# Attention and token mixing under one written order: all PSUM banks in one pool, groups of scores ordered singly, loads behind the first q and k

## The chip, the cores and the metric

The kernel runs on one core of one Trainium2 chip. The metric is the time of one execution on the device in microseconds. The kernel before took 212.9 us, the median of three runs (211.02, 212.9 and 214.1). Lower is better.

## What is computed

Two stages, fused. The first is attention over 4 batches, 8 heads, 768 positions and 64 channels, in which a query sees a window of 128 keys and the first 4 keys ("sinks"). The second is one layer of an MLP mixer over the result, read as 4 batches of 768 tokens by 512 channels.

```python
scores = (q @ k.transpose(0, 1, 3, 2)) / np.sqrt(D)          # D = 64
keep = (pos[None, :] < n_sink) | ((rel >= 0) & (rel < window))
a = softmax(np.where(keep, scores, -1e9))
x = (a @ v).transpose(0, 2, 1, 3).reshape(B, S, H * D)       # 4 x 768 x 512
h = np.maximum(x.transpose(0, 2, 1) @ w_tok1, 0) @ w_tok2    # 768 -> 256 -> 768
u = x + h.transpose(0, 2, 1)
out = u + np.maximum(u @ w_ch1, 0) @ w_ch2                   # 512 -> 1536 -> 512
```

All matrix work is in bf16 with sums in float32.

## The kernel before

**Pairs and batches.** Two heads make a pair, so there are 16 pairs, four of each batch. Only two tiles of 128 keys reach a tile of 128 queries, and the four sinks are added as a small matmul of their own.

**Units.** The work of TensorE (PE) is cut into units, and each unit belongs to a stream that is named by a letter. The first attention (pairs 0 to 3) has t (transposition of q or k), m (the additive mask, put into PSUM by a matmul), s (scores), o (sinks' scores and the products with v, `pv`, L686); g and h are the token mixing of batch 0. Pairs 4 to 15 and the token mixing of batches 1 to 3 are made in `attention_and_tokens` (L948) as streams a and k. c holds the 96 units of the first channel product (`v1`, L990, 4 matmuls of 384 columns each), x the units of the second (`whole`, L1145, 3 matmuls of 512 columns each, 24 units in a batch).

In stream a, units are bursts (L408): several pieces joined into one unit. For pair p one burst holds the transposition of pair p + 1 (`transposed`, L544, up to pair 7), scores of group 0 (`scores`, L583) and the sinks' part of the output of pair p - 1 (`sink_values`, L728); two units `values` (L762) follow; a second burst holds scores of groups 1 and 2, and in some pairs the sinks' scores (`score_sinks`, L659) or the transposition of u (`turned_u`, L879). Pieces use parts of the array: transposition, scores of group 0 and the sinks' values 64x128, scores of groups 1 and 2 and turned u 64x64, the sinks' scores 64x32; all other units use the whole array.

Below, "S8,0" is the scores of pair 8, group 0, and "V8" the values of pair 8; "k8", "v8" name loads.

**The order.** ORDERED (L47) is the order of all units on PE. LOADED (L60) is the order of the loads that POOL issues: q, k and v of a pair, w_tok (t0, t1), w_ch1 in four parts (c0 to c3) and w_ch2 in four (d0 to d3). q and k of a pair take two DMAs each. q and k of pairs 0 to 3 are loaded in float32 by SP and cast (on ACT, DVE and, for pair 3, POOL); all other loads cast on their way and are issued by POOL.

**The planner.** `Plan` (L279) runs while the program is built. It walks through ORDERED, and with costs in ns (L251 and in each `Op`) estimates when each unit and each piece of other work could run. From that it chooses the engine and the place in the engine's queue of every eviction, exponential, copy, load and DMA transposition. What is put into an engine's queue runs in that order on the chip: a copy that waits for a late load holds up all that stands behind it on its engine. `ready` (L289) is the time at which what an operation needs is done; `choose` (L304) gives a unit its PSUM banks; `other` (L336) takes the operation that can begin first. Loads are taken in the order of LOADED, with at most 8 DMAs in flight.

**PSUM.** There are eight banks. Before, two pairs of banks (sc, `NSC = 2`) are for scores and masks, and four single banks (mx, `NMX = 4`) for all else. Once the units of the first attention and token mixing are over, mx units may take halves of the sc tiles too (`late`).

**From pair 8 on** (BY_DMA) q and k are transposed by DMAs that SP issues (`turn` in `prepare`, L452), and four columns of each kT are copied to kTs (`sinks_of`, POOL or DVE). `sink_rows` (L776) copies the four sink rows of v of each pair to v_sink; ACT, DVE or POOL may do it. For pairs 0 to 3 one copy, `v_sink` (POOL, after a small load on SP), does this; the load v1 waits for that copy in the planner (L1270), and so do those behind v1 in LOADED; t0 and q4 stand ahead of it.

Of the kernel before, what the change touches and what calls it, by code (L numbers as in the profile page):

```python
# [16 lines left out]
def kernel(  # L17
# [41 lines left out]
    SC_LATE = 0  # L59
# [19 lines left out]
    NSC, NMX = 2, 4  # L79
    LATER = "cxyak"  # L80
# [5 lines left out]
    def bank(tag, *shape, dtype=FP32, slot=None):  # L86

        n = given[tag].pop(0) if slot is None else slot
        if tag == "sc":
            return sc[n]  # L90
        if n < 2 * NSC:
            size = 1
            for x in shape:
                size *= x
            flat = sc[n // 2][:, n % 2].rearrange("p b c d -> p (b c d)")
            flat = (flat if dtype == FP32 else flat.bitcast(dtype))[:, 0:size]
            names = "abc"[:len(shape)]
            return flat.rearrange(
                f"p ({' '.join(names)}) -> p {' '.join(names)}", **{x: v for x, v in zip(names, shape)},
            )  # L100
        return psum.tile([P, *shape], dtype, name=f"ps_{tag}", tag=f"{tag}{n}", bufs=1)
# [79 lines left out]
    keep_warm(7, 2 * NSC)  # L181
# [69 lines left out]
    SEM = 90.0  # L251
    PE_OUT = 190.0
# [10 lines left out]
    class Op:  # L263
        def __init__(self, cost, fn, deps=(), then=(), size=0.0, lag=None, loads=0, traffic=0.0):
            self.cost, self.fn, self.deps, self.then = cost, fn, list(deps), list(then)
            self.done = None
            self.lag = SEM if lag is None else lag
            self.size = size
            self.urgent = 0
            self.loads, self.traffic = loads, traffic  # L270
            self.need = {}
            self.half = False

# [5 lines left out]
    class Plan:  # L279
        def __init__(self):  # L280
            self.free = {"PE": 0.0, "ACT": 0.0, "DVE": 0.0, "SP": 0.0, "POOL": 0.0}
            self.queue, self.landings = 0.0, []
            self.sent = 0.0
            self.half = False
            self.pending = []
            self.held = [()] * (2 * NSC + NMX)
            self.late = False

        def ready(self, op):  # L289
# [6 lines left out]
            return t  # L296
# [7 lines left out]
        def choose(self, op):  # L304

            taken, given, t = set(), {}, 0.0
            for tag in ("sc", "mx"):
                banks = op.need.get(tag, ())
                free = []
                if tag == "sc" and banks:  # L310
                    for n in range(NSC):
                        halves = [self.freed(2 * n), self.freed(2 * n + 1)]
                        if None not in halves:
                            free.append((max(*halves, self.free["PE"]), n))
                elif banks:
# [7 lines left out]
                given[tag] = [f[-1] for f in free[:len(banks)]]  # L323
                t = max([t] + [f[0] for f in free[:len(banks)]])
# [45 lines left out]
        def run(self, units, early):  # L370

            early = len(early)
            units = list(units)
            while units or self.pending:
                self.late = early == 0
# [18 lines left out]
                name, op = units.pop(0)  # L394
                self.commit_pe(op, t)
                early -= name not in LATER

# [54 lines left out]
    def prepare(p):  # L452
# [23 lines left out]
        if p >= BY_DMA:  # L476
# [23 lines left out]
            )  # L500
            plan.pending.append(done["kTs", p])
# [274 lines left out]
    def sink_rows(p):  # L776
# [5 lines left out]
        done["vs", p] = Op({"ACT": 550.0, "DVE": 420.0, "POOL": 600.0}, both, [done["v", p], done["pv", p - NHP]])  # L782
# [165 lines left out]
    def attention_and_tokens():  # L948

        tokens, units = [], []  # L950
        first, last = NHP, len(pairs) - 1
        prepare(first)
        units += [turn(first, n) for n in range(2)]
        for p in range(first, last + 1):
            b, hp = pairs[p]
            pieces = []
            if p < last:
                prepare(p + 1)
                if p + 1 < BY_DMA:
                    pieces.append(transposed(p + 1))  # L960
            pieces.append(scores(p, 0))
            if p > first:
                pieces.append(sink_values(p - 1))
            units.append(burst(*pieces))
            if p > first:
                units += [values(p - 1, i) for i in range(2)]
            pieces = [scores(p, 1), scores(p, 2)]
            if hp == 0 and p > first:
                tokens.append(mix_h(b - 1, 1, 0, NTOK))
                tokens += [mix_u(b - 1, 1, st, 2) for st in range(0, NT, 2)]  # L970
                if p <= BY_DMA:
                    pieces.append(turned_u(b - 1, 1))
            if hp == NHP - 1 and p < BY_DMA:
                pieces.append(turned_u(b, 0))
            if hp % 2 == 0:
                pieces.append(score_sinks(p + 1))
            units.append(burst(*pieces))
            units[-1].then.append(sink_rows(p))
            if hp == 2:
                tokens.append(mix_h(b, 0, 0, NTOK))  # L980
                tokens += [mix_u(b, 0, st, 2) for st in range(0, NT, 2)]
        units += [pv(p, half) for half in range(2)]
        tokens.append(mix_h(b, 1, 0, NTOK))
        tokens += [mix_u(b, 1, st, 2) for st in range(0, NT, 2)]
        return units, tokens
# [284 lines left out]
    loads["v1"][1].deps.append(v_sink)  # L1270
    for name in LOADED.split():
        queue(*loads[name])
# [40 lines left out]
    streams.update(zip("ak", attention_and_tokens()))  # L1313
# [9 lines left out]
    plan.run(units, [u for u in units if u[0] not in LATER])  # L1323
# [35 lines left out]
```

## Time and profile before

| what | before |
|---|---|
| runs shown, us | 211.02, 212.9, 214.1 (median 212.9) |
| profiled execution, us | 211.98 |
| its span, first to last instruction, us | 210.2 |
| TensorE busy, us | 196.1 (93%) |
| ScalarE (ACT) busy, us | 106.1 (50%) |
| VectorE (DVE) busy, us | 103.4 (49%) |
| GpSimd (POOL) busy, us | 73.1 (35%) |
| moved by DMA | 26.28 MB, mean 125 GB/s |
| mean granted clock of TensorE | 0.984 |

The profile is of one execution. The page lists busy time by engine and by 40 slices of the span; the digits are tenths of a slice, and PEclk is the clock that TensorE was granted, in tenths of full speed. The view of stretches gives the same by windows of time. The waits say which engine sat idle for what, with the total in us, the count and the longest. The chain of waits follows the work that ended last back from the end; in order of time its columns are start, length and what ran. A row of a timeline has start, length, engine, line, operation, tiles (out<-in), shapes and count, and in brackets the idle time of the engine ahead of it and what ended it. Line numbers such as L147 are often those of a helper through which all matmuls go, so rows are told apart by their tiles.

### The profile page before, as it was taken

How to read it: one execution, taken by the hardware profiler on the slowest of the kernel's cores; microseconds unless marked ns; L12 is line 12 of the kernel's file. 1: busy time of each engine (PE TensorE's matmuls, PEld its weight loads, DVE VectorE, ACT ScalarE, POOL GpSimd, SP SyncE). 2: the span in 40 equal slices, each digit the busy share in tenths (PEclk: the TensorE clock that was granted, in tenths of full speed). 3: DMA queues.
4: the chain of work that ended last, by engine and by line, in shares of the span. 5: the costliest groups of instructions: out<-in, count | busy, mean ns of one | idle time of the engine just before them, and what ended most of it. 6: DMA issues, size and time to landing. Idle time of an engine off the chain costs nothing.

```text
span 210.2 us, 4834 instructions
## 1 busy us (share of the span) xinstructions
PE 196.1 (93%) x1999; PEld 117.7 (56%) x2017; DVE 103.4 (49%) x228; ACT 106.1 (50%) x184; POOL 73.1 (35%) x110
## 2 busy tenths in 40 slices
PE   6686999999999999929999999999999999999993
PEld 2333688666664655615765655567665455565453
DVE  4666677676496656614656657753422322000222
ACT  4496768877864115347776425458553003774000
POOL 7667967688364967554310040000000000000000
PEclk9999799999999999978999999999999999999999
DMA  6999999999999999999945763220120533000222
GB/s 173 247 282 162 155 167 195 173 157 195 120 175 128 174 229 183 173 155 182 152 53 100 90 159 93 90 57 23 25 50 3 150 102 119 8 0 0 100 103 100
DMA packets 92550, 26.28 MB, mean 125 GB/s; under 512 B 82544, under 2 KB 89584, under 8 KB 92528
## 3 DMA queue, kind: packets, MB, share of 16 engines
q0 software_dynamic: 67232, 11.80, 75.4%
q1 hardware_dynamic: 25296, 14.17, 29.3%
q8 instruction: 16, 0.26, 0.5%
q14 instruction: 6, 0.05, 0.1%
HBM read 26.75 MB, written 6.29 MB: 157 GB/s over the span
## 4 chain that ended last, share of the span: by engine, by line
PE 75%; DMA 16%; POOL 4%; issue 1%; DVE 1%; ACT 0%
PE ps_mx L147 65%; DMA v_aug<-in_v_dram 10%; PE ps_sc L147 9%; DMA q_bf<-in_q_dram 6%; POOL q_bf L132 1%; POOL v_aug L140 1%; PE ps_mx L552 1%; PE ps_mx L150 1%; PE ps_mx L534 0%; POOL w_tok L165 0%; DVE u_sb L856 0%; POOL mask_add L197 0%; POOL mask_add L201 0%; ACT v1T L160 0%; DVE mask_add L191 0%
## 5 line engine op out<-in xcount | busy, mean ns | idle before, releaser
L147 PE MATMUL ps_mx<-uT,w_ch 128*128 128x384 bf16 x364 | 66.1, 331 | 3.7 <-ACT v1T L160 3.7
L147 PE MATMUL ps_mx<-w_ch,v1T 128*128 128x512 bf16 (+2 forms) x285 | 62.8, 361 | 0.9 <-issue 0.2
L160 ACT ACTIVATE v1T<-ps_mx 128x384 bf16<-128x384 f32 x78 | 38.2, 493 | 36.3 <-PE ps_mx L147 34.7
L623 ACT ACTIVATE pT<-ps_sc 128x1024 bf16<-128x1024 f32 (+1 forms) x48 | 44.5, 953 | 19.0 <-PE ps_sc L147 18.6
L147 PEld LDWEIGHTS <-w_ch 128*128 128x128 bf16 x384 | 36.6, 99 | 28.3 <-issue 6.0
L147 PEld LDWEIGHTS <-v1T 128*128 128x128 bf16 x312 | 28.5, 98 | 27.5 <-issue 0.5
L1158 DVE TENSOR_TENSOR o_sb<-ps_mx,u_sb 128x512 f32<-128x512 f32 x22 | 15.2, 691 | 36.1 <-PE ps_mx L147 36.0
L132 POOL DMA_DIRECT2D k_bf<-in_k_dram x24 | 19.9, 834 | 8.6 <-DMA k_bf<-in_k_dram 4.0
L147 PEld LDWEIGHTS <-w_tok 128*128 128x128 bf16 x192 | 18.5, 98 | 5.5
L132 POOL DMA_DIRECT2D q_bf<-in_q_dram x24 | 19.9, 837 | 4.6 <-DMA w_ch<-in_moe_w_ch_dram 2.2
L856 DVE TENSOR_TENSOR u_sb<-ps_mx,x_sb 128x512 bf16<-128x512 f32 x19 | 12.9, 689 | 15.4 <-PE ps_mx L147 15.2
L140 POOL DMA_DIRECT2D v_aug<-in_v_dram x16 | 16.6, 1043 | 9.1 <-ACT v1T L160 3.6
L641 DVE TENSOR_TENSOR pT<-pT,mask_main 128x1024 bf16<-128x1024 bf16 (+1 forms) x24 | 14.4, 619 | 6.4 <-ACT pT L623 6.4
L147 PEld LDWEIGHTS <-pT 128*128 128x128 bf16 x352 | 15.3, 100 | 3.3 <-DMA v_aug<-in_v_dram 0.4
L147 PE MATMUL ps_sc<-qT,kT 64*64 64x192 bf16 (+3 forms) x288 | 15.6, 256 | 0.0
L147 PE MATMUL ps_mx<-v_aug,pT 128*128 128x65 bf16 x308 | 15.0, 197 | 0.0
L147 PE MATMUL ps_mx<-h1T,w_tok 128*128 128x256 bf16 x92 | 13.8, 273 | 0.0
L147 PE MATMUL ps_mx<-x_sb,w_tok 128*128 128x256 bf16 x96 | 11.9, 273 | 0.1
L147 PEld LDWEIGHTS <-kT 64*64 64x64 bf16 (+1 forms) x288 | 6.8, 103 | 8.7 <-issue 6.7
L641 DVE TENSOR_TENSOR pT<-pT,mask_first 128x1024 bf16<-128x1024 bf16 x13 | 8.9, 684 | 5.3 <-ACT pT L623 5.1
L162 DVE TENSOR_SCALAR v1T<-ps_mx 128x384 bf16<-128x384 f32 x13 | 7.2, 555 | 7.2 <-PE ps_mx L147 7.0
L156 POOL COPY kTs<-kT 64x4 bf16<-64x4 bf16 x14 | 2.6, 184 | 23.2 <-DMA kT<-k_bf 18.8
(79 smaller groups left out, 150.5 us busy)
## 6 DMA issues: line engine op xcount, KB each, us to landing
out_dram<-o_sb SPq DMA_DIRECT2D x23, 256.0 KB, 2.2
v_aug<-in_v_dram POOLq DMA_DIRECT2D x16, 192.0 KB, 9.0
w_ch<-in_moe_w_ch_dram POOLq DMA_DIRECT2D x8, 384.0 KB, 9.2
q_bf<-in_q_dram POOLq DMA_DIRECT2D x24, 96.0 KB, 8.4
k_bf<-in_k_dram POOLq DMA_DIRECT2D x24, 96.0 KB, 9.7
q_f<-in_q_dram SPq DMA_DIRECT2D x4, 384.0 KB, 6.7
k_f<-in_k_dram SPq DMA_DIRECT2D x4, 384.0 KB, 7.6
w_tok<-in_moe_w_tok_dram POOLq DMA_DIRECT2D x2, 384.0 KB, 9.6
```

The source lines that it names most:

```text
L132: in_order(nc.gpsimd.dma_start(out=out[:, h], in_=rows[:, h]))
L140: in_order(nc.gpsimd.dma_start(out=v_aug.rearrange("p i t d -> p (i t) d")[:, :, 0:D], in_=v[b].rearrange("h s d -> (h s) d")[2 * hp * S:2 ...
L147: in_order(nc.tensor.matmul(*args, skip_group_check=True, **kwargs))
L150: in_order(nc.tensor.transpose(out, in_, ident))
L156: in_order({"DVE": nc.vector, "POOL": nc.gpsimd}[e].tensor_copy(out=out, in_=in_))
L160: in_order(nc.scalar.activation(out, in_, AF.Relu))
L162: in_order(nc.vector.tensor_scalar_max(out=out, in0=in_, scalar1=0.0))
L552: in_order(nc.tensor.transpose(ps[x][:, n, j], bfs[p, n][rows, j], ident[rows, rows]))
L623: in_order(nc.scalar.activation(part(tiles["pT", p][:, :, ds(2 * g, 2)]), of_keys(tiles["ps_s", p, g])[:, :, 0:width(g)], AF.Exp, scale=scale,
L641: in_order(nc.vector.tensor_tensor(out=pt, in0=pt, in1=m, op=ALU.min))
L856: in_order(nc.vector.tensor_tensor(out=u_part(b, g, s0, n), in0=tiles["ps_u", b, g, s0], in1=x_sb[b][:, s0:s0 + n, c0:c0 + cn], op=ALU.add,))
L1158: in_order(nc.vector.tensor_tensor(out=o_sb.rearrange("p (g c) -> p g c", g=2), in1=u_rows(b, st), in0=tiles["ps_out", b, st].rearrange("p ...
```

## The change

- `NSC = 4` and no `NMX`: all eight banks are four tiles of two banks. A unit of scores or masks takes a tile, and any other unit takes any free bank. `choose` prefers banks that have been free for SLACK (250 ns); scores take low ones first, others high ones. `late`, `LATER` and `SC_LATE` go.
- `attention_and_tokens` returns five streams in place of two: a (scores, each group a unit of its own, 36), b (for each two pairs the sinks' scores, and for each pair the sinks' values and two units of values, 42), e (transpositions of pairs 4 to 7), f (turned u of batch 1) and k (token mixing, as before). The last pair uses sink_values and values in place of two `pv` units. The sink rows of all pairs, and the preparation of all pairs, are put before the planner at the start.
- ORDERED and LOADED are new. All loads of LOADED wait for the v_sink copy in the planner.
- In the planner, an operation can have a margin that is added to the time at which it is ready: 1500 ns for sink_rows, 1000 ns for the kTs copies from pair 8 on. Stores and transpositions by DMA now push back the estimated queue of loads by their full cost, not by 0.6 of it. sink_rows looks up the values unit of four pairs earlier by its name at the time it is needed.

```diff
     ORDERED = (
-        "t0-1 m0-1 s0-1 t2-3 m2 s2 m3 o0 s3 m4 t4 o1 s4 m5 t5 o2 s5 m6 t6 s6 a0 m7 t7 s7 o3 m8 s8 o4 s9-10 a1 m9 "
-        "g0 s11 m10 o5 s12 o6 g1 o7-8 a2 g2-3 h0-1 g4-5 h2-3 a3 g6 h4-7 g7 c0-3 a4 c4-5 a5-6 c6-9 a7 c10-14 a8-10 "
-        "c15-19 k0 a11 c20 k1 c21-23 k2 a12 k3 a13-14 x0-2 a15 x3-7 a16 x8 a17 x9 a18 x10-12 k4 x13-14 k5-6 x15 "
-        "k7 x16-19 a19 x20-23 c24 a20 c25 a21 c26 a22 c27 a23 c28-34 a24-25 c35-36 a26-27 c37 k8 c38-40 k9 c41-42 "
...
+        "t0-1 m0-1 s0 m2 s1 t2-3 s2 m3 s3 m4 o0 s4 m5 t4 s5 o1 t5 o2 m6 t6 s6 o3 m7 t7 s7 m8 o4 s8-10 m9-10 "
+        "s11-12 g0 o5-6 g1 o7-8 g2 e0-1 g3 h0-1 g4-5 h2-3 g6 h4-5 g7 h6 e2 a0 h7 c0-2 b0 a1 c3-5 b1 a2-3 c6-8 b2 "
+        "c9 a4-5 c10-12 b3 c13-14 e3 b4 c15-16 b5 c17 b6 c18-19 e4 a6-7 k0 c20 x0 b7 a8 c21-22 k1 x1 a9 b8 c23 b9 "
+        "k2 x2 b10 a10-11 x3-8 a12-13 b11-13 x9-11 k3 x12 k4 x13 a14 f0 a15 b14 x14 k5-6 x15-17 k7 x18-20 f1 a16 "
+        "b15 x21-22 c24-27 x23 c28 b16 c29-30 b17 c31-34 a17 b18 a18 c35-37 b19-20 c38-39 a19-20 b21 c40-43 k8 "
...
     LOADED = (
-        "t0 q4 v1 k4 k5 v2 q5 v3 t1 v4 k6 c1 c0 c2 q6 v6 d0 k7 q7 v5 q10 q8 c3 d2 d3 k8 q9 d1 v7 k9 k10 q11 q12 "
-        "q13 v12 v8 k11 v10 k13 k15 v9 q14 q15 k12 v11 v13 v14 k14 v15"
+        "v1 t0 v3 v2 t1 q4 k4 c3 q5 c0 k5 c2 v4 d1 k7 k6 v5 c1 q6 q7 d0 v6 q8 d2 k9 k8 v7 d3 q9 k11 v8 q13 k10 v9 "
+        "k15 v12 q10 k14 q11 k12 q12 v10 v11 v13 q14 v14 k13 q15 v15"
     )
...
-    NSC, NMX = 2, 4
-    LATER = "cxyak"
+    NSC = 4
...
-            return t
+            return t + op.margin
...
+            ats = [self.freed(n) for n in range(2 * NSC)]
...
-                        halves = [self.freed(2 * n), self.freed(2 * n + 1)]
+                        halves = ats[2 * n:2 * n + 2]
                         if None not in halves:
-                            free.append((max(*halves, self.free["PE"]), n))
+                            free.append((max(max(halves) + SLACK, self.free["PE"]), n, max(halves)))
                 elif banks:
-                    for n in range(2 * SC_LATE if self.late else 2 * NSC, 2 * NSC + NMX):
-                        at = self.freed(n)
+                    for n, at in enumerate(ats):
                         if at is not None and n not in taken:
-                            free.append((max(at, self.free["PE"]), n < 2 * NSC, at, n))
+                            free.append((max(at + SLACK, self.free["PE"]), 2 * NSC - 1 - n, at))
...
-                        self.queue = max(self.queue, self.free["SP"]) + 0.6 * op.traffic
+                        self.queue = max(self.queue, self.free["SP"]) + op.traffic
...
+            done["kTs", p].margin = 1000.0
             plan.pending.append(done["kTs", p])
...
-        done["vs", p] = Op({"ACT": 550.0, "DVE": 420.0, "POOL": 600.0}, both, [done["v", p], done["pv", p - NHP]])
+        done["vs", p] = Op({"ACT": 550.0, "DVE": 420.0, "POOL": 600.0}, both, [done["v", p], ("pv", p - NHP)])
+        done["vs", p].margin = 1500.0
         return done["vs", p]
...
+        scored, out, turns, turned, tokens = [], [], [], [], []
+        first, end = NHP, len(pairs)
+        for p in range(first, end):
+            prepare(p)
+            plan.pending.append(sink_rows(p))
+        turns += [turn(first, n) for n in range(2)]
+        turns += [burst(transposed(p)) for p in range(first + 1, BY_DMA)]
+        for p in range(first, end):
+            scored += [burst(scores(p, g)) for g in range(NT // 2)]
+            if p % 2:
+                out.append(burst(score_sinks(p)))
+                for n in (p - 1, p):
+                    out += [burst(sink_values(n)), *(values(n, i) for i in range(2))]
...
-    loads["v1"][1].deps.append(v_sink)
     for name in LOADED.split():
+        loads[name][1].deps.append(v_sink)
         queue(*loads[name])
```

The orders not printed here in full end alike: the second channel product of batch 3 comes last in both.

More of the change, by code (lines that the diff above doesn't have):

```diff
@@ L90, in bank @@
             return sc[n]
[L91 to L101, printed above, removed]
+        size = 1
+        for x in shape:
+            size *= x
+        flat = sc[n // 2][:, n % 2].rearrange("p b c d -> p (b c d)")
+        flat = (flat if dtype == FP32 else flat.bitcast(dtype))[:, 0:size]
+        names = "abc"[:len(shape)]
+        return flat.rearrange(
+            f"p ({' '.join(names)}) -> p {' '.join(names)}", **{x: v for x, v in zip(names, shape)},
+        )
     in_order = tc.keep_in_program_order
@@ L251 @@
     SEM = 90.0
+    SLACK = 250.0
     PE_OUT = 190.0
@@ L322, in choose @@
                     return None, None
-                given[tag] = [f[-1] for f in free[:len(banks)]]
-                t = max([t] + [f[0] for f in free[:len(banks)]])
+                found = free[:len(banks)]
+                t = max([t] + [f[2] for f in found])
+                given[tag] = [f[1] if tag == "sc" else 2 * NSC - 1 - f[1] for f in found]
                 if tag == "sc":
@@ L368, in commit_pe, with run @@
             self.pending.extend(op.then)
[L370 to L372 removed]
+        def run(self, units):
             units = list(units)
             while units or self.pending:
[L375 removed]
                 o = self.other()
@@ L393, in run @@
                 assert t is not None, "no unit can begin"
-                name, op = units.pop(0)
-                self.commit_pe(op, t)
-                early -= name not in LATER
+                self.commit_pe(units.pop(0)[1], t)
     def unit(ns, fn, deps=(), need=None, then=(), half=False):
@@ L948, in attention_and_tokens @@
     def attention_and_tokens():
[L950 to L981, printed above, removed]
@@ L987, in mix_channels @@
+        return scored, out, turns, turned, tokens
     def mix_channels(b):
@@ L1322 @@
         units += [(name, streams[name][n]) for n in range(int(first), int(last or first) + 1)]
-    plan.run(units, [u for u in units if u[0] not in LATER])
+    plan.run(units)
 _INS = ['q', 'k', 'v', 'n_sink', 'window', 'moe_w_tok1', 'moe_w_tok2', 'moe_w_ch1', 'moe_w_ch2']
```

19 lines of the change are left out of this document (10 added, 9 removed), and 9 rows, old and new, of the table ORDERED.

## The prediction

> **What bounds the kernel now.** I read the page first, then the stretches, then the waits and the chain in order of time, and last the timelines of ACT, POOL and PE at the places the chain pointed to. The page:
>
> ```profile
> span 210.2 us, 4834 instructions
> PE 196.1 (93%) x1999; PEld 117.7 (56%) x2017; DVE 103.4 (49%) x228; ACT 106.1 (50%) x184; POOL 73.1 (35%) x110
> ...
> PEclk9999799999999999978999999999999999999999
> DMA  6999999999999999999945763220120533000222
> ```
>
> TensorE is the bound: busy 93% of the span, and no other engine is above 56%. The DMA row matters as much: the DMA engines are nine tenths busy from the second slice (5.3 us) to the twentieth, so for the first half of the span the loads are a second bound, and an order that asks for a load too soon waits. The PEclk row has two dips, in the fifth slice and in the eighteenth and nineteenth. The stretches show what stands there:
>
> ```profile
> 15.00:20.00 5.00, 3.13 (x65) 1.86 (x65) 3.18 (x10) 3.76 (x6) 3.17 (x4) 1.00 2.16 185
> 20.00:25.00 5.00, 5.00 (x71) 2.67 (x69) 3.19 (x9) 2.69 (x4) 4.82 (x7) 0.66 2.26 147
> ...
> 85.00:90.00 5.00, 4.40 (x58) 2.71 (x57) 2.91 (x7) 1.40 (x2) 2.38 (x4) 1.00 1.56 171
> 90.00:95.00 5.00, 1.91 (x7) 0.89 (x7) 1.00 (x2) 2.96 (x7) 3.18 (x4) 0.74 2.11 164
> 95.00:100.00 5.00, 5.00 (x52) 3.07 (x51) 2.05 (x5) 3.31 (x7) 2.03 (x6) 0.92 2.28 174
> ```
>
> The columns are the stretch, its length, busy time of PE, PEld, DVE, ACT and POOL, and the granted clock. PE loses time before 20 us and around 90 us, and each loss is followed by a stretch at a lower clock. From 25 us on, outside 88 to 97, PE is full. The waits name the two losses:
>
> ```profile
> PE ps_mx L147 <- ACT v1T L160: 3.7, 1, 3.7
> PE ps_mx L534 <- DMA q_bf<-in_q_dram: 1.6, 1, 1.6
> ...
> PE ps_sc L147 <- ACT pT L623: 0.2, 1, 0.2
> ```
>
> **Loss A, at 18 us.** Unit a0 turns q of pair 4 and stands in PE's order before the end of the first attention. Its load is late:
>
> ```profile
> 6.32 13.16 DMA q_bf<-in_q_dram
> 19.47 0.14 issue
> 19.61 0.35 PE ps_mx L534 x12
> ```
>
> PE waits 1.6 us, and then runs 20 to 25 at a clock of 0.66, which costs (1 - 0.66) x 5 = 1.7 us. Together 3.3 us.
>
> **Loss B, at 89 us.** On ACT, in order of time:
>
> ```profile
> 86.63 0.49 ACT L160 ACTIVATE v1T<-ps_mx 128x384 bf16<-128x384 f32 x1 [0.72 <-PE ps_mx L147]
> 92.00 0.53 ACT L154 ACTIVATE v_sink<-v_aug 4x65 bf16<-4x65 bf16 x2 [4.88 <-DMA v_aug<-in_v_dram]
> 92.55 0.49 ACT L160 ACTIVATE v1T<-ps_mx 128x384 bf16<-128x384 f32 x1
> ```
>
> ACT took up the copy of sink rows of v (sink_rows, L776) before that load had landed, and sat 4.88 us. Behind it in ACT's queue stood the eviction of a PSUM bank for which PE waited. The load is that of pair 9: its issue is the twelfth of v, and v9 is the twelfth v in LOADED:
>
> ```profile
> 80.91 1.01 POOL L140 DMA_DIRECT2D v_aug<-in_v_dram x1 [0.69 <-DMA v_aug<-in_v_dram]
> ```
>
> The wait costs PE 3.7 us. The lower clock adds (1 - 0.74) x 1.91 x 2 = 1.0 us at 93 to 95 (busy time that ran at half rate there) and 0.08 x 5 = 0.4 us after 95. Together 5.1 us.
>
> **The change, part by part.** Matrix work is the same but for the last pair (two pv units become sink_values and values, under 0.2 us, counted as nothing).
>
> *LOADED.* v9 moves from place 41 of 49 to place 34, v8 from 36 to 31, while the units that use them (V9, V8) stand after nearly the same work as before. SLACK, the margins of 1500 (sink rows) and 1000 (kTs), and the full cost of transposes and stores in the planner's queue move those copies later on their engines. I take loss B as gone: -5.1 us. What is late next is in the rivals.
>
> *The start.* a0 becomes e0, and moves behind the first attention, g1 and g2. Loss A goes, up to -3.3 us, but the loads allow less. v1, t0 and the rest now wait for the v_sink copy (L156 on POOL, 9.12 to 9.73). Before, t0 and q4 were issued ahead of it, from 4.69:
>
> ```profile
> 4.69 0.83 POOL L165 DMA_DIRECT2D w_tok<-in_moe_w_tok_dram  x1
> 5.50 1.75 POOL L132 DMA_DIRECT2D q_bf<-in_q_dram  x2
> 9.12 0.61 POOL L156 CAST v_sink<-v_sink_f 128x520 bf16<-128x520 f32 x1 [1.86 <-DMA v_sink_f<-in_v_dram]
> ...
> 18.43 1.02 POOL L140 DMA_DIRECT2D v_aug<-in_v_dram  x1
> ...
> 44.32 2.25 POOL L165 DMA_DIRECT2D w_ch<-in_moe_w_ch_dram  x3
> ```
>
> On POOL's queue some five loads fit between 9.73 and the cast of q_f of pair 3 (at 16.23, where POOL idled 2.2 us), so that cast is not put off. The pace of loads: I count a load of v, or of a pair's q or k, as one share (192 KB) and a weight as two (384 KB). From v2 (18.43) to c3 (44.32) 22 shares went out in 25.9 us, 1.18 us each. With three shares (t0, q4) in by 19.5, and the same volume (v1, t0) then if the engines are as full as before, the new list has k5 (place 11, 15 shares) in at 19.5 + 12 x 1.18 = 33.6 and c1 (place 18, 25 shares) at 45.4. The users: e2 stands 5.6 us of PE work later than a2, which held the same transposition:
>
> ```profile
> 29.85 0.46 PE ps_mx L552 x24
> ...
> 38.14 0.65 PE ps_mx L147 x4
> ...
> 46.61 3.38 PE ps_mx L147 x20
> ```
>
> (thirteen units of g and h that ran behind a2 now run ahead), so e2 comes at 35.4 less the gain; c12, the third of the five v1 units in the last row (47.9), has 1.0 us less work ahead (the transposition of pair 6 and one values unit now come behind it), and comes at 46.9 less the gain. So k5 allows a gain of 1.8 us and c1 one of 1.5. My pace counts a weight as two full shares, which is too dear for weights, so both land a little sooner. I take -2.0 us, between 1.5 and 3.3.
>
> *Single groups.* Bursts joined pieces of one tiling of the array. I counted changes between the shapes 128x128, 64x128, 64x64 and 64x32 along both orders: 84 before, 90 after (full to small 75 and 67; among the small ones 9 and 23). Price, from the same 16 score matmuls:
>
> ```profile
> 56.05 0.49 PE L147 MATMUL ps_sc<-qT,kT 64*64 64x192 bf16 x16
> 56.47 0.40 PE L147 MATMUL ps_mx<-qT,kTs 64*32 64x512 bf16 x4
> ...
> 63.98 0.49 PE L147 MATMUL ps_sc<-qT,kT 64*64 64x192 bf16 x16
> 64.28 0.60 PE L522 MATMUL ps_mx<-ident,u_sb 64*64 64x64 bf16 x48
> ```
>
> Before a change of shape they take 0.42 us from start to start, before work of the same shape 0.30: 0.12 us a change. Of the 14 more changes among small shapes all are between 64x128 and 64x64, a pair that has no row here. If they are free the sum is -8 x 0.12 = -1.0 us; at the nearest row's price it is 6 x 0.12 = +0.7 us. I take +0.7, as the change to 64x32 is as much a change among small shapes. The Trainium skill speaks against this part of the change: its page "TensorEngine Tiling (Array Packing)", section "Tiling Modes", says that a change of tiling mode, not merely of tile, drains TensorE. By that rule every one of the 14 is paid, +0.7 us; the row to 64x32 agrees with it, and for the pair in question no run here shows it yet.
>
> *One pool of banks.* PE's waits before hold one of 0.2 us for a bank of scores and loss B, so at most 0.2 us is to be won. The cost: sink_values now takes two banks until its values units have run (b15 to b17 is 7 us of work), and c24 to c27 and c72 to c75 hold four until the last unit of the batch before has read v1T. Eight banks cover both by my count; if not, PE waits for one eviction of 0.5 us at each. I take zero.
>
> *Sum.* 210.2 - 5.1 - 2.0 + 0.7 = 203.8 us of span. The profiled execution took 211.98 us, 1.8 more than its span, so 205.6 us. It lies 0.9 below the median of the runs shown (212.9); I leave that, since its two losses are DMA waits that differ from run to run.
>
> **The rivals.**
>
> *kT of pair 8 is late.* k8 is the 26th load in both lists, after equal shares (35), so it lands near 19.5 + 32 x 1.18 = 57.3 in both. S8,0 (a16 before, a12 after) has 0.3 us less work ahead:
>
> ```profile
> 68.16 0.39 PE L147 MATMUL ps_sc<-qT,kT 64*128 64x256 bf16 x4
> ...
> kT<-k_bf SPq DMA_TRANSPOSE x8, 6.8
> ```
>
> With the gain it comes at 65.9. The transposition takes 6.8 us in the median, and k9 now lies ahead of k8: 57.3 + 6.8 = 64.1, and one more transposition ahead of it makes it 65 to 68. A wait of 2 us, with a stretch at half clock of 1 us or so, gives 208.5 us. Before, it was hidden by 2 us; 20%.
>
> *The loads start late.* If the DMA engines were not full from 5 to 10 us without t0 and q4, their three shares are lost: 3 x 1.18 = 3.5 us, the gain at the start turns into a loss, and the time is 209.1 us. For it: every load of the list waits for 9.73. Against: q_f and k_f fill the engines then (first slice six tenths, with hardly another load). 15%.
>
> *Nothing mended.* Another sink copy blocks ACT as v9's did: 205.6 + 5.1 = 210.7 us. Each batch has four such copies. 5%.
>
> *Slower: POOL's own queue.* POOL copies kTs after a DMA transposition, and loads are issued behind it:
>
> ```profile
> POOL kTs L156 <- DMA kT<-k_bf: 18.8, 4, 7.7
> ```
>
> and the chain has S10,0 at
>
> ```profile
> 97.80 0.33 PE ps_sc L147 x4
> ```
>
> Before, most of these waits came after the last load. In the new list 23 loads stand behind k8. If POOL takes the copies of pairs 9, 8, 10 and 11 and sits 6.8 us at each, of which the loads in flight cover about half, the list slips by 4 x 3.4 = 13.6 us. q10 (47 shares: 71.4, with some 10 us of transposes and stores 81, and its own transposition 87) then comes at 101 for S10,0 at 90 (97.8 in the row, less loss B, 0.3 and 2.0), and PE waits 11 us and runs slow for 1.7: 218 us. It decides once the list slips by more than 3 us, and makes a slower kernel from 15. Against: the copies have a margin and may go to DVE. 10%.
>
> **How the numbers follow.** Forecast (202.5 to 207.5) 50%, kT8 20%, late loads 15%, nothing mended 5%, POOL 10%. The low end is the sum with free changes (-1.7) and the whole of loss A (-1.3). The range goes from 202.5 to 211.0: it leaves out POOL and little else. About 2% is what a measurement of this kernel can tell from no change: 208.6 and 217.2. Faster: the forecast, three fifths of kT8, a fifth of late loads, 65%. Slower: POOL, 10%. Within: 25%.
>
> **What would show it.** Right: no wait of ACT for v_aug over 1 us before 100 us; no PE wait for q_bf near 18 us and a clock of 1.00 from 20 to 25; the first c unit (38.1 before, and 1.1 us less work ahead now) at 36 or less; PE without a gap over 0.5 us from 25 us to the end. Wrong: a PE gap over 2 us anywhere, with a lower clock behind it; PE waiting for k_bf, w_ch or kT; POOL idle over 3 us for kT ahead of a load; small gaps at each single group that sum to over 2 us.

## The result and the profile after

The changed kernel takes 232.72 us (median of 4 runs, 232.21 to 233.13); the kernel before, beside it on the same chip, 211.96 us (4 runs, 210.84 to 214.1). The ratio is 1.0998 with an interval of 1.0916 to 1.1079: 10% slower. Ratios here leave out executions that ran disturbed, so they need not be the quotient of the two medians.

The profiled execution of the changed kernel took 232.35 us, its span 230.6. Its page:

```profile
span 230.6 us, 4854 instructions
PE 200.3 (87%) x2003; PEld 115.5 (50%) x2021; DVE 107.6 (47%) x240; ACT 100.2 (43%) x176; POOL 71.6 (31%) x106
...
PE   6878987999899989999998988998888798888872
...
PEclk9999999999999999999999999999999999999999
DMA  6999999999999999999077351002104211001212
```

The clock is full in every slice, both dips of before are gone, and yet PE is busy for only 87% of the span (93% before). The row of PE shows where: eights and nines are mixed from end to end, and the second half, where the DMA engines have little to do, is the worse one. The stretches of the changed kernel (columns as in the prediction; the two behind the clock are of the DMA engines):

```profile
15.00:20.00 5.00, 4.12 (x75) 2.44 (x75) 2.85 (x10) 3.88 (x8) 5.00 (x7) 1.00 1.89 177
20.00:25.00 5.00, 4.34 (x68) 3.35 (x68) 2.26 (x5) 3.08 (x4) 4.11 (x7) 1.00 1.91 176
25.00:60.00 35.00, 31.41 (x406) 20.32 (x404) 21.92 (x53) 22.32 (x43) 26.92 (x35) 1.00 1.90 169
...
90.00:95.00 5.00, 4.62 (x46) 2.80 (x44) 2.16 (x5) 1.98 (x5) 1.02 (x2) 1.00 2.02 130
...
100.00:150.00 50.00, 46.41 (x486) 27.13 (x490) 28.23 (x59) 24.19 (x42) 2.93 (x11) 1.00 0.65 90
150.00:200.00 50.00, 43.42 (x281) 24.15 (x283) 14.26 (x26) 13.97 (x29) 0.00 (x0) 1.00 0.17 48
```

From 15 to 25 and from 90 to 95, where before had its two losses, the clock stands at 1.00, and from 90 to 95 PE does 4.62 us of work instead of 1.91. The loss is elsewhere: 3.6 us of idle time from 25 to 60, 3.6 from 100 to 150, 6.6 from 150 to 200. Before, the last two stretches had 0.4 and 0.2 us of it:

```profile
100.00:150.00 50.00, 49.63 (x546) 31.08 (x548) 30.02 (x62) 28.66 (x45) 4.84 (x17) 1.00 0.52 85
150.00:200.00 50.00, 49.79 (x279) 27.52 (x282) 10.05 (x15) 17.82 (x36) 0.00 (x0) 1.00 0.19 59
```

The waits of PE in the changed kernel (total, number, longest):

```profile
PE ps_sc L145 <- DVE o_sb L1139: 6.4, 9, 0.8
PE ps_sc L145 <- ACT v1T L158: 4.6, 12, 0.7
PE ps_sc L145 <- DVE u_sb L853: 3.2, 6, 0.8
```

No wait is long and none is for a load of weights, of k or of kT. PE waits for readers of PSUM: the sum into o_sb, the eviction to v1T, the sum into u_sb. None of these waits is much over 0.8 us; one such reading takes 0.69 us on DVE and 0.49 us on ACT. The end of the kernel, where nothing runs but the last channel product, shows one at a time (timeline of the changed kernel, PE and DVE):

```profile
207.33 5.34 PE L145 MATMUL ps_sc<-w_ch,v1T 128*128 128x512 bf16 x24
...
209.53 0.69 DVE L1139 TENSOR_TENSOR o_sb<-ps_sc,u_sb 128x512 f32<-128x512 f32 x1 [16.17 <-PE ps_sc L145]
...
212.77 0.69 DVE L1139 TENSOR_TENSOR o_sb<-ps_sc,u_sb 128x512 f32<-128x512 f32 x1 [2.55 <-PE ps_sc L145]
213.51 2.75 PE L145 MATMUL ps_sc<-w_ch,v1T 128*128 128x512 bf16 x11 [0.84 <-DVE o_sb L1139]
...
216.30 0.69 DVE L1139 TENSOR_TENSOR o_sb<-ps_sc,u_sb 128x512 f32<-128x512 f32 x1 [2.84 <-PE ps_sc L145]
```

Twelve matmuls make one row tile of the output, and a row tile has a bank of its own. From 209 us on, DVE has nothing to do but to add up finished row tiles. Yet it does not begin when a row tile is finished: it begins when PE's run of matmuls ends (212.67, then 216.26), and PE goes on only when DVE is done (213.46). The compiled program names the PSUM tile. These are four of DVE's instructions in their order, with what each reads and waits for (the brackets name the engines and queues waited for):

```
231 L1139 TensorTensor o_sb_2786<-ps_sc_88,u_sb 128x512 [waits DVE_49,DMAHW4_49,PE_49,Activation_49]
232 L1139 TensorTensor o_sb_2801<-ps_sc_88,u_sb 128x512 [waits DMAHW6_49,DVE_49,PE_49]
233 L1139 TensorTensor o_sb_2816<-ps_sc_88,u_sb 128x512 [waits DMAHW7_49,DVE_49,PE_49]
234 L1139 TensorTensor o_sb_2840<-ps_sc_88,u_sb 128x512 [waits DMAHW0_49,DVE_49,PE_49]
```

The row tiles at the end use the two banks of one tile, ps_sc_88, in turn. In the program's list for PE, the first of the stretches above is 9 matmuls into ps_sc_87 and 15 into ps_sc_88: the last nine of one row tile, all twelve of the next, and three of the one after. Only then does DVE read the row tile that was finished three matmuls earlier, and the fourth matmul of the new one waits for that reading. So PE stops in the middle of a sum, with its own bank in hand: it waits for no free bank. Two engines that use different banks of one tile take turns.

### The profile page after: what moved, and what is told of

It is laid out like the page before. It is cut to its first block, busy times and chain, and to the rows that moved or that the text cites. A ratio compares the mean times of both kernels' runs of the same rounds, so it can differ in the third digit from the quotient of the medians.

```text
span 230.6 us, 4854 instructions
## 1 busy us (share of the span) xinstructions
PE 200.3 (87%) x2003; PEld 115.5 (50%) x2021; DVE 107.6 (47%) x240; ACT 100.2 (43%) x176; POOL 71.6 (31%) x106
## 4 chain that ended last, share of the span: by engine, by line
PE 66%; DVE 14%; ACT 9%; DMA 5%; issue 3%; SPq 0%; POOL 0%; DVEq 0%; POOLq 0%; ACTq 0%
PE ps_sc L145 65%; ACT v1T L158 6%; DVE o_sb L1139 4%; DMA v_aug<-in_v_dram 3%; DVE u_sb L853 3%; DMA v_sink_f<-in_v_dram 2%; DVE v1T L160 2%; DVE x_sb L746 1%; DVE x_sb L706 1%; ACT pT L619 1%; ACT u_sb L152 1%; DVE pT L637 1%; ACT pT_sink L671 1%; DVE h1T L160 0%; ACT uT L152 0%
## 5 line engine op out<-in xcount | busy, mean ns | idle before, releaser
L145 PE MATMUL ps_sc<-w_ch,v1T 128*128 128x512 bf16 (+2 forms) x297 | 68.1, 362 | 10.2 <-DVE o_sb L1139 5.5
L145 PE MATMUL ps_sc<-uT,w_ch 128*128 128x384 bf16 x384 | 70.2, 326 | 5.9 <-ACT v1T L158 3.4
L158 ACT ACTIVATE v1T<-ps_sc 128x384 bf16<-128x384 f32 x78 | 35.5, 491 | 60.4 <-PE ps_sc L145 48.2
L145 PEld LDWEIGHTS <-w_ch 128*128 128x128 bf16 x384 | 36.1, 97 | 31.8 <-issue 9.6
L1139 DVE TENSOR_TENSOR o_sb<-ps_sc,u_sb 128x512 f32<-128x512 f32 x23 | 15.8, 689 | 50.7 <-PE ps_sc L145 50.7
L145 PE MATMUL ps_sc<-v_aug,pT 128*128 128x65 bf16 x352 | 16.0, 193 | 1.7 <-DMA v_aug<-in_v_dram 0.7
L853 DVE TENSOR_TENSOR u_sb<-ps_sc,x_sb 128x512 bf16<-128x512 f32 x20 | 13.4, 682 | 7.5 <-PE ps_sc L145 6.3
L145 PE MATMUL ps_sc<-qT,kT 64*64 64x192 bf16 (+3 forms) x288 | 15.8, 251 | 0.1
L746 DVE TENSOR_TENSOR x_sb<-ps_sc,recip 128x384 bf16<-128x384 f32 x24 | 13.3, 555 | 4.1 <-PE ps_sc L145 3.6
L160 DVE TENSOR_SCALAR v1T<-ps_sc 128x384 bf16<-128x384 f32 x18 | 9.8, 552 | 10.7 <-PE ps_sc L145 5.8
L145 PE MATMUL ps_sc<-h1T,w_tok 128*128 128x256 bf16 x96 | 14.4, 272 | 0.2 <-DVE u_sb L853 0.2
L145 PE MATMUL ps_sc<-x_sb,w_tok 128*128 128x256 bf16 x96 | 12.0, 273 | 0.0
```

The costliest lines, as they stand in the source:

```text
L145: in_order(nc.tensor.matmul(*args, skip_group_check=True, **kwargs))
L158: in_order(nc.scalar.activation(out, in_, AF.Relu))
L160: in_order(nc.vector.tensor_scalar_max(out=out, in0=in_, scalar1=0.0))
L746: in_order(nc.vector.tensor_tensor(out=x_sb[b][:, :, ds((2 * hp + i) * D, D)], in0=tiles["ps_o", p, i][:, :, 0:D], in1=tiles["recip", p, i ...
L853: in_order(nc.vector.tensor_tensor(out=u_part(b, g, s0, n), in0=tiles["ps_u", b, g, s0], in1=x_sb[b][:, s0:s0 + n, c0:c0 + cn], op=ALU.add,))
L1139: in_order(nc.vector.tensor_tensor(out=o_sb.rearrange("p (g c) -> p g c", g=2), in1=u_rows(b, st), in0=tiles["ps_out", b, st].rearrange("p ...
```

## The experiments

**The theories.** *Tiles:* the program's waits are set by PSUM tile and not by bank. The changed kernel keeps all eight banks in four tiles of two, so PE's writes into one bank wait for DVE's or ACT's reading of the other bank of that tile, and the reading waits for the writes. Before, this touched only the scores' tiles; nearly all other units had tiles of one bank. *Banks are short* (rival): single groups and sink_values hold banks for longer, eight are not enough, and the old split would wait as well. *The order* (rival): the new order itself makes PE run into its own evictions.

**e1_single_banks.** The changed kernel, with eight tiles of one bank; scores take two of them, so their exponential becomes two instructions. The planner, the order and the choice of banks stay.

```diff
-    sc = [psum.tile([P, 2, 2, 4, D], FP32, name=f"ps_sc{n}", tag=f"sc{n}", bufs=1) for n in range(NSC)]
+    sc = [psum.tile([P, 2, 4, D], FP32, name=f"ps_sc{n}", tag=f"sc{n}", bufs=1) for n in range(2 * NSC)]
...
-            return sc[n]
+            return sc[2 * n:2 * n + 2]
...
-        flat = sc[n // 2][:, n % 2].rearrange("p b c d -> p (b c d)")
+        flat = sc[n].rearrange("p b c d -> p (b c d)")
...
-            in_order(nc.scalar.activation(
...
+            for i in range(2):
+                in_order(nc.scalar.activation(
```

> The changed kernel with its eight banks as eight tiles of one bank in place of four tiles of two. The planner, the order, the loads and the choice of banks stay as they are. Only the exponential of a group of scores becomes two instructions, one for each bank. Theory (the two halves of one tile wait for each other, so PE waits for readers of a bank that it doesn't write, and readers wait for PE's writes to the other bank): 201 to 207 us, the gaps of 0.3 to 0.8 us go, and the gain at the start and the missing stall at 89 us are left. Rival one (eight banks are too few for the new order, or singly ordered groups cost this much): 225 us or more. Rival two (tiles that live for the whole program are slower than tiles taken anew by each unit): 225 us or more.

Measured: 207.56 us (206.68 to 208.58), ratio to before 0.9812 (0.9766 to 0.9858). That is 25 us less than the changed kernel. The waits of PE that are left in e1_single_banks, after its first 25 us, are for two loads; beside them stand five pauses of about 0.2 us that end with no wait:

```profile
PE ps_sc L145 <- DMA kT<-k_bf: 2.6, 1, 2.6
...
PE ps_sc L548 <- DMA k_bf<-in_k_dram: 1.5, 1, 1.5
```

and the same place in the last channel product looks like this (timeline of e1_single_banks):

```profile
187.54 12.69 PE L145 MATMUL ps_sc<-w_ch,v1T 128*128 128x512 bf16 x58
...
189.74 0.69 DVE L1140 TENSOR_TENSOR o_sb<-ps_sc,u_sb 128x512 f32<-128x512 f32 x1 [14.03 <-issue]
...
192.33 0.69 DVE L1140 TENSOR_TENSOR o_sb<-ps_sc,u_sb 128x512 f32<-128x512 f32 x1 [1.90 <-PE ps_sc L145]
194.87 0.69 DVE L1140 TENSOR_TENSOR o_sb<-ps_sc,u_sb 128x512 f32<-128x512 f32 x1 [1.84 <-PE ps_sc L145]
```

PE runs 58 matmuls in one piece while DVE reads finished row tiles beside it (three of the readings are shown). The order and the number of banks are as in the changed kernel, so neither rival holds. The median lies half a microsecond above the expected range.

**e2_old_pool.** The changed kernel with the pool of before: two tiles of two banks for scores, four single banks for the rest.

```diff
-    NSC = 4
+    NSC, NMX = 2, 4
+    LATER = "cxabefk"
+    SC_LATE = 0
...
+        return psum.tile([P, *shape], dtype, name=f"ps_{tag}", tag=f"{tag}{n}", bufs=1)
```

> The changed kernel with the pool of before: two pairs of banks for scores and masks, four single banks for all else, halves of the pairs for other units only after the first attention. Order, loads, margins and singly ordered groups are those of the changed kernel. Theory (halves of one tile wait for each other): 202 to 210 us, a little above the eight single tiles, as units still share the two pairs late. Rival one (order or singly ordered groups): 225 us or more. Rival two (tiles that live for the whole program): 202 to 210 us.

Measured: 210.03 us (208.17 to 211.6), ratio 0.992 (0.9886 to 0.9954). The new order with the old banks is a little faster than before, and 2.5 us slower than with eight single banks. What PE waits for here is banks and their evictions, in a few places (waits of PE in e2_old_pool):

```profile
PE ps_mx L149 <- DVE u_sb L862: 2.0, 1, 2.0
PE ps_sc L149 <- ACT pT L628: 1.8, 3, 1.1
PE ps_mx L149 <- ACT kTs L156: 1.7, 1, 1.7
```

So one pool seems to help the new order, once its tiles are single banks. Which part of it helps was not told apart: e2 also lacks SLACK and the preference for high or low banks, and its late units still share the two tiles of scores.

**e3_paired_mx and e4_single_mx.** The kernel before, order and plan untouched. In e3 its four single banks become two tiles of two banks. In e4, the control, they become four tiles of one bank that, as in e3, live for the whole kernel.

```diff
+    sc += [psum.tile([P, 2, 2, 4, D], FP32, name=f"ps_mx{n}", tag=f"mx{n}", bufs=1) for n in range(NMX // 2)]
...
-        return psum.tile([P, *shape], dtype, name=f"ps_{tag}", tag=f"{tag}{n}", bufs=1)
```

```diff
+    mx = [psum.tile([P, 1, 2, 4, D], FP32, name=f"ps_mx{n}", tag=f"mx{n}", bufs=1) for n in range(NMX)]
...
-        return psum.tile([P, *shape], dtype, name=f"ps_{tag}", tag=f"{tag}{n}", bufs=1)
```

> The kernel before, with its plan, order and loads as they are; only its four single banks become two tiles of two banks that live for the whole program. Theory (halves of one tile wait for each other): 217 to 232 us, with gaps of 0.3 to 0.8 us on PE. Rival one (the new order is the cause): within 1 us of before, 211 to 213. Rival two (tiles that live for the whole program): slower, and as slow as the run with four such tiles of one bank.

> The kernel before, with its plan, order and loads as they are; its four single banks become four tiles of one bank that live for the whole program, the control to the paired ones. Theory (halves of one tile wait for each other): within 1 us of before, 211 to 213. Rival one (the new order): the same. Rival two (tiles that live for the whole program): slower by 5 us or more.

Measured: e3 236.37 us (236.2 to 237.86), ratio 1.1188 (1.1139 to 1.1237); e4 211.27 us (208.9 to 214.28), ratio 0.99 (0.9842 to 0.9957). Putting the four banks of before into two tiles costs 25 us by itself, and its waits are those of the changed kernel (waits of PE in e3_paired_mx):

```profile
PE ps_mx L146 <- ACT v1T L159: 5.4, 13, 1.0
PE ps_mx L146 <- DVE o_sb L1157: 4.4, 6, 0.8
PE ps_mx L146 <- DVE u_sb L855: 2.1, 4, 0.8
```

That is 4 us more than the upper end of what was expected for e3. Tiles that live throughout cost nothing (e4). With e1 and e3 the cause is shown from both sides: take the pairing out of the kernel after and 25 us go, put it into the kernel before and 25 us come.

**e5_k8_first.** e1_single_banks showed the rival that the prediction priced: kT of pair 8 late. Here k8 is loaded ahead of d2 and k9.

```diff
-        "... v6 q8 d2 k9 k8 v7 d3 q9 ..."
+        "... v6 q8 k8 d2 k9 v7 d3 q9 ..."
```

> Eight tiles of one bank, and in the list of loads k8 moves two places forward, ahead of d2 and k9, so that SP issues the transposition of kT of pair 8 ahead of that of pair 9. Theory (with the pool out of the way, what is left of the loss is that transposition, queued on SP behind the one of pair 9: a wait of 2.6 us for kT and some 1.7 us at half clock behind it): the wait at S8,0 goes, 202 to 204.5 us. Rival (PE only meets the next late load a little later): within 1 us of the run with eight tiles, 206.5 to 208.5 us, with another wait of 2 us or more for a load.

Measured: 206.14 us (205.56 to 207.2), ratio 0.9731 (0.9674 to 0.9787), the lowest median of the study, but above the 202 to 204.5 us expected. Its runs and its interval overlap those of e1_single_banks, so a gain over it is not shown by the times. The wait for kT is gone; the rows of S8,0 in the timelines of PE, first e1_single_banks, then e5_k8_first:

```profile
63.76 0.38 PE L145 MATMUL ps_sc<-w_ch,v1T 128*128 128x512 bf16 x1
66.71 0.88 PE L145 MATMUL ps_sc<-qT,kT 64*128 64x256 bf16 x12 [2.58 <-DMA kT<-k_bf]
```

```profile
60.75 4.04 PE L145 MATMUL ps_sc<-w_ch,v1T 128*128 128x512 bf16 x18 [0.26 <-DMA w_ch<-in_moe_w_ch_dram]
64.72 0.68 PE L145 MATMUL ps_sc<-qT,kT 64*128 64x256 bf16 x12
```

Its profiled execution is 2.8 us shorter than that of e1, and lost some time early, at half clock from 15.1 to 18.5 us. Of PE's waits in it only that for `ones` (1.5 us, in every kernel here) and one for q_bf at 12 us (1.1 us) are above 0.9 us.

**e6_early_loads.** e1_single_banks with t0 and q4 at the head of LOADED and not behind the v_sink copy, as before the change.

```diff
-        "v1 t0 v3 v2 t1 q4 k4 c3 ..."
+        "t0 q4 v1 v3 v2 t1 k4 c3 ..."
...
-        loads[name][1].deps.append(v_sink)
+        if name not in ("t0", "q4"):
+            loads[name][1].deps.append(v_sink)
```

> Eight tiles of one bank, with t0 and q4 put back at the head of the list of loads and freed from the wait for the sink rows of v, as in the kernel before. Theory (the loads of the list, issued by then, take DMA time from the float32 q and k of pairs 0 to 3, and put off the first attention): q_f and k_f of pair 3 land 1.5 to 3 us later than with all loads behind (13.7 and 14.9 us in the changed kernel), PE reaches the last scores of the first attention 1 to 3 us later, and the time is 1 to 3 us longer where nothing else is late. Rival (the gain at the start is that of the order alone, a0 moved behind the first attention): the last scores of the first attention within 0.5 us of the run with all loads behind.

Measured: 209.99 us (209.3 to 212.91), 2.4 more than e1_single_banks. PE waits for v1 instead (waits of PE in e6_early_loads), and runs at half clock from 19.2 to 26.0 us:

```profile
PE ps_sc L145 <- DMA v_aug<-in_v_dram: 3.2, 1, 3.2
```

The scores of the last group of pair 3 stand at 26.98 us here, at 20.11 in e1_single_banks, at 27.31 before. That is 6.9 us later than in e1, where 1 to 3 had been expected. Most of it is not q and k of the first attention but v1: it is issued at 9.0 us and PE has it at 20.1, while in e1 it is issued at 9.5 and PE has it at 15.8. Holding t0 and q4 back is what makes the start faster. Only 2.4 us of the 6.9 are left at the end; the waits of e1 for k5 and for kT of pair 8 do not come here.

**e7_no_margin.** e1_single_banks with margins of 0 for sink_rows and kTs and 0.6 of the traffic in the planner's queue, as before the change; the lists stay.

```diff
-            done["kTs", p].margin = 1000.0
+            done["kTs", p].margin = 0.0
...
-        done["vs", p].margin = 1500.0
+        done["vs", p].margin = 0.0
...
-                        self.queue = max(self.queue, self.free["SP"]) + op.traffic
+                        self.queue = max(self.queue, self.free["SP"]) + 0.6 * op.traffic
```

> Eight tiles of one bank, with both margins at 0 and the cost of transpositions and stores in the planner's queue back at 0.6. Theory one (the margins keep the copies of sink rows off engines that would wait): ACT or DVE sits idle for a load of v for 2 us or more before 100 us, and the time is 2 to 6 us longer than with margins. Theory two (the earlier places of v8 and v9 in the list are what ended the stall at 89 us): no idle of ACT or DVE for a load of v over 1 us, and the time within 2 us of the run with margins.

Measured: 213.32 us (210.14 to 215.59), ratio 1.0005 (0.9948 to 1.0062), where e1_single_banks has 0.9812; its shortest run is longer than the longest of e1_single_banks (208.58). Loss B is back. The rows of ACT's and PE's waits and the place, in the profiled execution of e7_no_margin (215.59 us, the longest of its runs):

```profile
ACT v_sink L152 <- DMA v_aug<-in_v_dram: 11.1, 3, 4.5
...
PE ps_sc L145 <- ACT v1T L158: 3.6, 2, 3.4
```

```profile
94.43 0.52 ACT L152 ACTIVATE v_sink<-v_aug 4x65 bf16<-4x65 bf16 x2 [4.08 <-DMA v_aug<-in_v_dram]
94.98 1.25 ACT L158 ACTIVATE v1T<-ps_sc 128x384 bf16<-128x384 f32 x3
```

ACT again sits at a copy of sink rows with three evictions behind it, and PE waits 3.4 us for one of them. The earlier places of v8 and v9 in the list do not prevent that by themselves; the later places in the engines' queues do. Whether the margins or the fuller count of traffic do more was not told apart.

**e8_k5_too.** e5_k8_first with k5 earlier too: c3 moves from ahead of q5 to behind c1.

```diff
-        "... t1 q4 k4 c3 q5 c0 k5 c2 v4 d1 k7 k6 v5 c1 q6 ..."
+        "... t1 q4 k4 q5 k5 c0 c2 v4 d1 k7 k6 v5 c1 c3 q6 ..."
```

> As the run with k8 ahead of d2 and k9, and c3 moves from ahead of q5 to behind c1, so that k5 lands earlier. Theory (PE waited 1.5 us for k5 at the transposition of pair 5): 201 to 203 us, 1 to 1.5 us less than with k8 alone. Rival (the loads are the bound there, and the wait moves on to the next load, c0 or v4): no difference to k8 alone within 0.5 us.

Measured: 206.91 us (206.31 to 207.22), ratio 0.9758 (0.9709 to 0.9807): no gain over e5_k8_first. The wait has moved to the next loads (waits of PE in e8_k5_too):

```profile
PE ps_sc L145 <- DMA w_ch<-in_moe_w_ch_dram: 1.6, 1, 1.6
...
PE ps_sc L530 <- DMA k_bf<-in_k_dram: 0.7, 1, 0.7
```

## Why the prediction was wrong, step by step

**The step that failed: "One pool of banks", taken as zero.** I counted banks, found that eight cover the longer holdings, and asked only whether a free bank would be late. I did not ask by what the program sets its waits. The change puts every bank into a tile with a neighbour, and c and x units, evicted all the time, then share tiles with each other. In the prediction's sum stands 0.0 us for it; measured, it is 232.7 - 207.6 = 25 us. The idle time from 25 us to the end of the span accounts for most of it: by the stretches 3.6 (25 to 60) + 2.6 (60 to 100) + 3.6 + 6.6 + 8.6 (200 to the end) = 25.0 us, against 9.6 us by the same sum in e1_single_banks. Another part is in PE's busy time (200.3 against 193.8 us): a matmul that ends a run is counted to its end, 0.38 us (the single one at 63.76 in e1_single_banks, above), where one inside a run takes some 0.22 (24 in 5.34 us), so each stop also hides about 0.16 us of draining in the busy time. The view of waits sums up 48 waits in the changed kernel and 12 in e1_single_banks; 36 x 0.16 = 5.8 us is an estimate for this part, of the 6.5 us by which the busy times differ. Of the 23.8 us between the two profiled spans, these two parts are 15.4 and 6.5 us; the other 2 us are idle time ahead of 25 us.

It could have been seen: the front part of this document says that all eight banks are four tiles of two, and that each other unit takes any free bank. The trace of before did hold units in halves of the scores' tiles, but so few that no wait came of it (groups of PE in the kernel before; the last column is idle time ahead of them):

```profile
L147 PE MATMUL ps_mx<-uT,w_ch 128*128 128x384 bf16 x364 | 66.1, 331 | 3.7 <-ACT v1T L160 3.7
...
L147 PE MATMUL ps_sc<-uT,w_ch 128*128 128x384 bf16 x20 | 4.1, 326 | 0.0
```

By the prediction's own way such a cost has to be bounded from both sides. The nearest row was the eviction of 0.5 us that it named; one for each of the 96 c units and the 24 row tiles is 60 us, and the range would have had to hold a slow case.

None of the rivals was this one. The list of signs had "small gaps at each single group"; small gaps came, but at evictions, and in e1_single_banks they are gone with the same single groups. The other half of the step, that at most 0.2 us is to be won, was read from waits under the old order; under the new one, eight single banks are 2.5 us faster than the old split (e2). The slower rival, POOL's queue, did happen in its first half: POOL waited for kT longer than before and issued the next loads late (POOL's waits and timeline in the changed kernel):

```profile
POOL kTs L154 <- DMA kT<-k_bf: 34.8, 6, 10.9
```

```profile
65.48 0.42 POOL L154 COPY kTs<-kT 64x4 bf16<-64x4 bf16 x2 [7.57 <-DMA kT<-k_bf]
66.06 1.64 POOL L130 DMA_DIRECT2D k_bf<-in_k_dram  x2 [0.16 <-issue]
```

Yet no wait of PE for a load after that followed, neither in the changed kernel nor in e1_single_banks, where POOL waits 30.5 us for kT. So the loads behind the block had more time in hand than I gave them.

**The other steps are read in e1_single_banks**, which is the change without the shared tiles. Its profiled span is 206.8 us against the 203.8 of the sum.

*LOADED and the margins: right.* By the signs that the prediction named, ACT has no wait for v_aug in either kernel, and the first c unit comes at 32.66 us in e1 and at 35.05 in the changed kernel (36 or less). The late load of loss B was named rightly, though v9 is the eleventh v of LOADED: v0, which is issued ahead of the list, makes it the twelfth load of v. Loss B is gone in the changed kernel and in e1. e7 shows which part of it does the work: the margins and the full traffic, not the list. The prediction named both and did not tell them apart. ACT's six copies of sink rows in the changed kernel wait for almost nothing (groups of the changed kernel; the last column is idle time ahead of them):

```profile
L152 ACT ACTIVATE v_sink<-v_aug 4x65 bf16<-4x65 bf16 x6 | 1.5, 251 | 0.1
```

*The start: right in kind, too small.* Loss A is gone, and PE is further ahead than the 2.0 us that I took. The last products with v of the first attention start at 23.4 us in e1 and at 29.6 before, where PE had by then also transposed q and k of pair 4 (0.6 us): 5.6 us ahead. Counted in the same work done, it is some 4.0 us at 60 us. Two reasons. The rival "loads start late" had its effect turned round: without t0 and q4 among them, the other loads land sooner. In the median from issue to landing, q of the first attention takes 5.7 us in the changed kernel (6.7 before) and k 6.3 us (7.6 before); e6 gives the gain back when those two loads go first, through v1 above all. The bound by k5 was right as a mechanism: k5 landed at 31.8 us (33.6 forecast, at a pace that counted weights too dear), and PE waited 1.5 us for it, the row of k_bf shown for e1_single_banks.

*Single groups: agrees.* 0.12 us for a change of shape was taken for pieces of 64x128 and 64x64, for which before had no row. In the changed kernel the sinks' values, eight matmuls of 64x128, take 0.13 us from start to start before scores of the same shape, and 0.22 us before scores of 64x64: 0.09 us a change (timelines of PE in the changed kernel):

```profile
41.01 0.30 PE L145 MATMUL ps_sc<-v_sink,pT_sink 64*128 64x65 bf16 x8
41.23 0.65 PE L145 MATMUL ps_sc<-qT,kT 64*64 64x192 bf16 x12
...
108.54 0.29 PE L145 MATMUL ps_sc<-v_sink,pT_sink 64*128 64x65 bf16 x8
108.67 0.67 PE L145 MATMUL ps_sc<-qT,kT 64*128 64x256 bf16 x12
```

So the rule of the Trainium skill that the prediction weighed (page "TensorEngine Tiling (Array Packing)", section "Tiling Modes") holds for this pair too, at a little less than the price taken.

*kT of pair 8: this rival is real, once the tiles no longer hide it.* In e1 S8,0 waits 2.6 us and PE then runs at half clock from 67.0 to 70.4. It was forecast at 2 us and about 1 us. kT came at 66.7 us, inside the 65 to 68 of the prediction; PE came sooner than the 65.9 us forecast, as the start gained more. In the changed kernel S8,0 comes at 70.2, after enough small stops that kT is there in time. In e5 this wait is gone, and the profiled span is 2.8 us shorter than in e1, less than the 2.6 plus about 1.7 us (half of 3.4) of the wait: its PE is 2.0 us behind at the end of the first attention (the last scores of pair 3). Whether that comes from the edit or from differences between executions stays open.

With the start at 4.0 in place of 2.0 us and kT at 4.3, the prediction's sum is 203.8 - 2.0 + 4.3 = 206.1 us of span, against 206.8 measured in e1.

## What to carry to other kernels

Before banks are pooled, ask at which grain the program keeps engines apart: where that is the tile, two banks in one tile are one bank with regard to waits, and PE and its readers take turns. A price that the trace of before can't show is bounded by the count of places at which it could be paid; a zero needs a row. When a profile shows no long wait but a busy share a few points lower at full clock, sum up the short waits of the bounding engine by what ended them.

## What the runs showed of the hardware

PE can write one bank of PSUM while DVE reads another without loss: 58 matmuls in one piece (12.69 us) with DVE's readings beside them, in e1_single_banks. The Trainium skill says so as well (page "PSUM — Partial Sum Buffer", section "Summary: rules for kernel authors"): read a different bank while matmuls run, and guard with semaphores by bank. The runs agree; what the changed kernel paid was for guards that are coarser than that.

What lowered the clock was neither the total of the waits nor the length of one gap. The changed kernel lost 23.7 us in 48 waits, of which only the first, for `ones`, is over 0.9 us, and kept a clock of 1.00 from 0 to 200 us. In e1 one gap of 2.6 us was followed by 3.4 us at half clock, and one of 1.5 us by none; before, one of 1.6 us was followed by a stretch at 0.66. But gaps of 1.96 us (e2, at 64 us) and 1.99 us (e4, at 19 us) were followed by none, and one of 1.07 us (e5, at 12.9 us) was. The trace of before shows a beat: its half clocks run from 20.67 to 24.09 and from 92.35 to 95.77 us, each 3.42 us long, and start 71.7 us apart, 21 times that length. In the 3.41 us just ahead of them PE was idle for 1.78 and 2.95 us, ahead of that in e1 for 2.58, in e2 for 1.60 and in e5 for 1.49. Cut along the same beat, the gap of 1.99 us in e4 is spread over two windows with 1.22 and 1.29 us of idle time, and that of 1.96 us in e2 over two with 0.94 and 1.07. So the idle time in one window of the beat fits these runs better than the length of a gap. It gives no sharp limit: windows with 1.54 us (e2), 1.58 us (e8) and 1.76 us (the end of e4) were followed by no half clock. The Trainium skill's page "TensorE: Matmul & The Clock Gate", section "What's actually happening", gives a window of about 3.4 us that runs on its own beat; the length of the half clock and the beat agree with it, while the gaps that brought it on here were shorter than a window.
